# Decode attention plus a gated MLP on one core: four-head tiles in five places against eight-head tiles in three

## The chip, the cores and the metric

One core of a Trainium2 chip runs the whole program. The metric is device time in microseconds (us), the median of three executions; lower is better. The profile is one further execution, read with the chip's hardware profiler. Engines are called PE (matrix), PEld (its weight loads), DVE (vector), ACT (scalar), POOL and SP; SP is here only the queue that issues the large transfers.

## The reference, cut to what matters

Four batch rows, one new token each, D = 640, 32 heads of 128, caches of 4,096 positions, all in bfloat16.

```
xn = layernorm(x)                                  # x: 4 x 1 x 640
q  = (xn @ wq) per head                            # wq: 640 x 4096
p  = softmax(q . k_cache / sqrt(128))              # k_cache: 4 x 32 x 4096 x 128
o  = p . v_cache                                   # v_cache: the same shape
A  = o @ wo                                        # wo: 4096 x 640
z  = gelu(xn @ w_in);  z1, z2 = halves of z        # w_in: 640 x 1728
B  = (z1 * (w_sp * layernorm(z2) + b_sp)) @ w_out  # w_out: 864 x 640
out = x + A + B
```

The two caches are 134 MB each. With wq, wo and the MLP's weights 282 MB have to be read, and every byte of the caches is used once.

## The kernel before, in words

A tile is the K or the V cache of four heads of one batch row: 4 x 4,096 positions x 128, laid on 128 lanes as 128 positions of 128 values each, 32 KB a lane, 4 MB in all. A lane holds positions of one head only, 32 lanes a head. There are 32 tiles of K and 32 of V, in the order head group by head group, four batch rows within each. They share a pool of five places of 32 KB a lane (`KV_SLOTS`); wq and the MLP's weights use three of the five first. `loads` is the fixed order of the transfers on SP's queue, and `pump()` issues the next as soon as the tile that had its place has been used.

The loop over `i` (32 turns) is an order written out by hand for PE, DVE, ACT and SP. Turn i works on the scores of K tile i, on the softmax of tile i - 1 and on a V tile one or more turns behind:

- `stage_q(i + 2)` spreads the query of the four heads over the lanes: four matmuls into four groups of 32 lanes (L389), and an ACT copy (L397).
- `product` (DVE, L403) multiplies a quarter of the K tile by that query into a tile `prod`, `fold_half` (DVE, L415) adds the upper 64 values of each position to the lower 64 into a tile `folded`, `sums` (PE, L427) adds eight-value pieces of a half tile with eight matmuls by the identity, and `row_sums` (DVE, L438) adds the last eight.
- For the softmax `lane_max`, `turn_max`, `head_max` and `spread_max` carry the largest score of each head across the lanes, and `exps` (ACT, L480) makes one exponential a head, each on that head's own 32 lanes, into a tile `p_m` that was zeroed at the start. Each also gives the sum of its values.
- `weighted` (PE, L495) loads each of the 128 positions of the V tile as weights (128 x 128) and moves the four columns of `p_m` past them.
- After four batch rows `group_den`, `group_norm` and `group_proj` (L507 to L525) divide by the sums and multiply by that head group's rows of wo. wo comes in eight transfers (`load_wo`) of 1,280-byte runs, spread over the loop.

The scores tile `s_sb` has two buffers, so that the next tile's `row_sums` never meets the `exps` of the last. The last V tile comes in four pieces (`V_CUTS`).

Ahead of the loop wq is read in five transfers, four rows of each lane's five in one and the fifth row in four pieces, three of them spread (`SPREADS`, L96); then come w_in and w_out, and 160 matmuls by wq (L236) give the queries.

Of the kernel before, what the change touches and what calls it, by code (L numbers as in the profile page):

```python
# [15 lines left out]
KV_SLOTS = 5  # L16
EXTRA_K = (24, 28)
# [3 lines left out]
def kernel(  # L21
# [14 lines left out]
    nc = tc.nc  # L36
# [11 lines left out]
    HT = 4  # L48
# [4 lines left out]
    NQ = 4  # L53
    QC = NC // NQ
    HC = NC // 2
    HD2 = Dh // 2
    RW = 8
    SLOT = NC * Dh
    NFF = Fh // P
    NFC = NFF + 1  # L60
    FT = Fh - NFF * P
    NOH = D // 2

    const = ctx.enter_context(tc.tile_pool(name="const", bufs=1))
    kv = ctx.enter_context(tc.tile_pool(name="kv", bufs=KV_SLOTS))
    wop = ctx.enter_context(tc.tile_pool(name="wop", bufs=1))
    prod = ctx.enter_context(tc.tile_pool(name="prod", bufs=1))
    fold = ctx.enter_context(tc.tile_pool(name="fold", bufs=2))
    work = ctx.enter_context(tc.tile_pool(name="work", bufs=1))
    small = ctx.enter_context(tc.tile_pool(name="small", bufs=2))  # L70
    PSUM = bass.MemoryType.PSUM
    ps_s = ctx.enter_context(tc.tile_pool(name="ps_s", bufs=2, space=PSUM))
    ps_pv = ctx.enter_context(tc.tile_pool(name="ps_pv", bufs=2, space=PSUM))
    ps_m = ctx.enter_context(tc.tile_pool(name="ps_m", bufs=2, space=PSUM))
    ps_out = ctx.enter_context(tc.tile_pool(name="ps_out", bufs=1, space=PSUM))

    def slot(name):
        return kv.tile([P, SLOT], BF16, tag="kv", name=name)

    x_bf = const.tile([Bsz, D], BF16)
    nc.scalar.dma_start(out=x_bf[:], in_=A_x.flatten_outer_dims())

    wq_v = A_wq.rearrange("(p c) n -> p c n", c=DC)
    wq_parts = []
    t = slot("wq")[:, 0 : HT * HD].rearrange("p (c n) -> p c n", n=HD)
    nc.sync.dma_start(out=t, in_=wq_v[:, 0:HT, :])
    wq_parts += [(t, i) for i in range(HT)]
    assert DC == HT + 1  # L90
    SPREADS = (2, 4, 8)
    NW = HD // (len(SPREADS) + 1)
    t = slot("wq")[:, 0:HD]
    nc.sync.dma_start(out=t[:, 0:NW], in_=wq_v[:, HT, 0:NW])
    for g, k in enumerate(SPREADS, 1):
        nc.sync.dma_start(  # L96
            out=t[:, g * NW : (g + 1) * NW],
            in_=wq_v[:, HT, g * NW : (g + 1) * NW].rearrange("(b a) n -> a b n", a=k),
        )
    wq_parts.append((t.rearrange("p (c n) -> p c n", c=1), 0))  # L100
# [6 lines left out]
    w_sb = slot("w_sb")  # L107
# [15 lines left out]
    V_CUTS = (0, 64, 96, 112, NC)  # L123

    def load(which, i):
        cache, tiles = (A_k_cache, k_tiles) if which == "k" else (A_v_cache, v_tiles)
        t = slot("k_nat" if which == "k" else "v_nat")
        cuts = V_CUTS if (which, i) == ("v", NT - 1) else (0, NC)
        for c0, c1 in zip(cuts, cuts[1:]):
            nc.sync.dma_start(  # L130
                out=t[:, c0 * Dh : c1 * Dh], in_=kv_view(cache, i)[:, c0 * Dh : c1 * Dh]
            )
        tiles[i] = t[:].rearrange("p (c d) -> p c d", d=Dh)

    loads = [("k", 0), ("k", 1)]
    n_k = 2
    for i in range(NT):
        loads.append(("v", i))
        for _ in range(2 if i + 1 in EXTRA_K else 1):
            if n_k < NT:  # L140
                loads.append(("k", n_k))
                n_k += 1
    occupants = [("w", 0), ("w", 1), ("w", 2)] + loads
    used = set()
    n_loaded = [0]

    def pump():
        while n_loaded[0] < len(loads):
            at = n_loaded[0] + 3 - KV_SLOTS
            if at >= 0 and occupants[at] not in used:  # L150
                return
            load(*loads[n_loaded[0]])
            n_loaded[0] += 1

    wo_v = A_wo.rearrange("(j h p) n -> j p h n", p=P, h=HT)
    wo_tiles = {}

    def load_wo(j):
        wo_tiles[j] = wop.tile([P, HT, D], BF16, name="wo")
        if j == HG - 1:  # L160
            for hh in range(HT):
                nc.sync.dma_start(out=wo_tiles[j][:, hh, :], in_=wo_v[j][:, hh, :])
            return
        nc.sync.dma_start(out=wo_tiles[j][:], in_=wo_v[j])

    pump()


# [4 lines left out]
    nc.vector.tensor_copy(out=ident_f[:], in_=ident[:])  # L173
    ones_row = const.tile([1, P], FP32)
    nc.vector.memset(ones_row[:], 1.0)
    eps_tile = const.tile([P, 1], FP32)
    nc.vector.memset(eps_tile[:], eps)
    scale_row = const.tile([1, P], FP32)
    nc.vector.memset(scale_row[:], scale_qk)
    ones_sq = const.tile([P, P], FP32)  # L180
    nc.vector.memset(ones_sq[:], 1.0)

    NACC = 2
    p_m = [const.tile([P, NC, HT], BF16, name=f"pm{b}") for b in range(Bsz)]
    acc = [const.tile([P, HT, Bsz], FP32, name=f"acc{g}") for g in range(NACC)]
    for t in p_m + acc:
        nc.gpsimd.memset(t[:], 0.0)

# [5 lines left out]
    for i in range(NSTAT):  # L194
# [8 lines left out]
    xn_bf = work.tile([Bsz, D], BF16)  # L203
    nc.vector.tensor_scalar(
        out=xn_bf[:],
        in0=x_bf[:],
# [6 lines left out]
    xn_v = xn_bf[:].rearrange("b (p c) -> b c p", c=DC)  # L213
    NX = DC + len(SPREADS)
    xnT_ps = ps_m.tile([P, NX, Bsz], BF16, tag="m")
    for g, k in enumerate(SPREADS):
        xn_l = work.tile([Bsz, P], BF16, name=f"xn_l{g}")
        nc.vector.tensor_copy(
            out=xn_l[:].rearrange("b (a q) -> b a q", a=k),
            in_=xn_v[:, HT, :].rearrange("b (q a) -> b a q", a=k),  # L220
        )
        nc.tensor.transpose(
            out=xnT_ps[:, DC + g, :], in_=xn_l[:], identity=ident[:Bsz, :Bsz]
        )
# [4 lines left out]
    xnT = const.tile([P, NX, Bsz], BF16)  # L229
    nc.vector.tensor_copy(out=xnT[:], in_=xnT_ps[:])  # L230

    q_ps = ps_m.tile([P, H, Bsz], FP32, tag="m", name="q_ps")
    for h in range(H):
        for c in range(DC):
            t, i = wq_parts[c]
            nc.tensor.matmul(  # L236
                out=q_ps[:, h, :],
                lhsT=t[:, i, h * Dh : (h + 1) * Dh],
                rhs=xnT[:, c if c < HT or h * Dh < NW else DC + h * Dh // NW - 1, :],
                start=(c == 0),  # L240
                stop=(c == DC - 1),
            )
    qT = const.tile([P, H, Bsz], BF16)
    nc.vector.tensor_copy(out=qT[:], in_=q_ps[:])  # L244


# [16 lines left out]


    gm = {}
    for name in ("zz", "gw", "gt", "gz"):
        gm[name] = work.tile([P, 2, NFC, Bsz], FP32, name=name)
    nc.gpsimd.memset(gm["zz"][:], 0.0)
    gm["sq"] = work.tile([P, NFC, Bsz], FP32, name="sq")
# [4 lines left out]
    def gmlp():  # L274
        zz, gw, gt, gz, sq = (gm[n] for n in ("zz", "gw", "gt", "gz", "sq"))
        zT = ps_pv.tile([P, 2, NFC, Bsz], FP32, tag="pv", name="zT")
        for t in range(2):
# [13 lines left out]
        nc.vector.tensor_tensor(out=gw[:], in0=zz[:], in1=zz[:], op=ALU.mult)  # L291
        nc.vector.tensor_scalar(
            out=gw[:], in0=gw[:], scalar1=0.044715, scalar2=1.0, op0=ALU.mult, op1=ALU.add
        )
        nc.vector.tensor_tensor(out=gw[:], in0=gw[:], in1=zz[:], op=ALU.mult)
        nc.scalar.activation(
            out=gt[:], in_=gw[:], func=ACT.Tanh, scale=math.sqrt(2.0 / math.pi)
        )
        nc.vector.tensor_scalar(
            out=gt[:], in0=gt[:], scalar1=1.0, scalar2=0.5, op0=ALU.add, op1=ALU.mult  # L300
        )
        nc.vector.tensor_tensor(out=gz[:], in0=zz[:], in1=gt[:], op=ALU.mult)
        nc.vector.tensor_tensor(out=sq[:], in0=gz[:, 1, :, :], in1=gz[:, 1, :, :], op=ALU.mult)

        s_ps = ps_m.tile([1, 2 * Bsz], FP32, tag="m", name="ln_ps")
        for src, at in ((gz[:, 1, :, :], 0), (sq[:], Bsz)):
            for k in range(NFC):
                nc.tensor.matmul(
                    out=s_ps[:, at : at + Bsz],
                    lhsT=ones_sq[:, 0:1],  # L310
                    rhs=src[:, k, :],
                    start=(k == 0),
                    stop=(k == NFC - 1),
                )
# [5 lines left out]
        tmp_t = st[:, 4 * Bsz : 5 * Bsz]  # L320
        nc.vector.tensor_scalar(
            out=st[:, 0 : 2 * Bsz],
            in0=s_ps[:],
# [33 lines left out]
            out=sq[:],  # L357
# [5 lines left out]
            out=sq[:],  # L363
            in0=sq[:],
# [3 lines left out]
        nc.vector.tensor_tensor(out=gm["yT"][:], in0=gz[:, 0, :, :], in1=sq[:], op=ALU.mult)  # L368
# [12 lines left out]

    qbcs, scores, pvs = {}, {}, {}
    folds, sums_ps, maxes = {}, {}, {}

    def stage_q(i):
        hg, b = divmod(i, Bsz)
        qb_ps = ps_m.tile([P, Dh], FP32, tag="m", name="qbc_ps")
        for hh in range(HT):
            nc.tensor.matmul(  # L389
                out=qb_ps[hh * LN : (hh + 1) * LN, :],  # L390
                lhsT=qT[:, HT * hg + hh, b : b + 1].to_broadcast([P, LN]),
                rhs=ident[:],
                start=True,
                stop=True,
            )
        qbcs[i] = small.tile([P, Dh], BF16, name="qbc", bufs=3)
        nc.scalar.copy(out=qbcs[i][:], in_=qb_ps[:])  # L397

    prods = {}

    def product(i, q):
        t = prods[i, q] = prod.tile([P, QC, Dh], BF16, name="prod")
# [134 lines left out]
    def at(i, fn, *args):  # L537
        if 0 <= i < NT:
            fn(i, *args)
# [101 lines left out]
```

## Time and profile before

| what | value |
|---|---|
| median of three executions | 682.32 us (682.05 to 682.57) |
| profiled execution, first to last instruction (span) | 680.6 us |
| read from memory | 282.2 MB, 415 GB/s over the span |
| large transfers' share of 16 DMA engines | 97.9% |
| DVE busy | 507.6 us (75%) |
| PE busy | 394.1 us (58%), at a mean granted clock of 0.627 |
| ACT busy | 94.3 us (14%) |

The profiled execution gives its span alone; the median lies 1.7 us above it, which is what lies around the span. The page shows the span in 40 slices of 17.0 us. Only the first two and the last move clearly less than 419 to 433 GB/s. A line Lnnn is that of the kernel before unless it is said to be of the kernel after.

### The profile page before, as it was taken

What the parts mean: (1) busy time and instruction counts of PE and PEld (TensorE: products, weight loads), DVE (VectorE), ACT (ScalarE), POOL (GpSimd) and SP (SyncE); (2) the same over time, 40 slices, a digit from 0 to 9 for tenths busy, and PEclk for the clock granted to TensorE, in tenths of its full rate; (3) what the DMA queues carried; (4) which work ended last, traced back from release to release, by engine and by line L of the source; (5) the groups of instructions that cost most, each with busy time, mean ns of one, the idle gap of its engine ahead of it and who ended that gap; (6) DMA issues with size and microseconds to landing.
All of it is one profiled execution on the core that took longest, in us unless ns stands there. A gap on an engine that the chain in (4) does not pass through costs nothing.

```text
span 680.6 us, 11504 instructions
## 1 busy us (share of the span) xinstructions
PE 394.1 (58%) x5196; PEld 214.0 (31%) x5196; DVE 507.6 (75%) x436; ACT 94.3 (14%) x329; POOL 2.8 (0%) x13
## 2 busy tenths in 40 slices
PE   1234766684555666554565745566655557645486
PEld 1221333332223333322333322333333224323155
DVE  1059987778777778797777887777786999876950
ACT  0110211111110111111011111101111111110120
POOL 1000000000000000000000000000000000000000
PEclk9999566666566556566656665755565665656565
DMA  8999999999999999999999999999999999999993
GB/s 312 340 429 433 427 429 428 419 431 431 429 430 425 428 430 431 421 432 432 429 430 423 429 429 430 427 427 430 429 432 424 428 430 427 428 432 430 433 409 130
DMA packets 15082, 282.98 MB, mean 416 GB/s; under 512 B 1358, under 2 KB 5562, under 8 KB 6458
## 3 DMA queue, kind: packets, MB, share of 16 engines
q1 hardware_dynamic: 15014, 282.25, 97.9%
q8 instruction: 40, 0.66, 0.4%
q14 instruction: 8, 0.07, 0.0%
q10 hardware_dynamic: 20, 0.01, 0.0%
HBM read 282.24 MB, written 0.01 MB: 415 GB/s over the span
## 4 chain that ended last, share of the span: by engine, by line
DMA 55%; DVE 25%; PE 16%; SPq 2%; issue 1%; DVEq 0%
DMA k_nat<-in_A_k_cache_dram 55%; DVE prod L403 14%; PE s_ps L427 9%; DVE folded L415 7%; PE pv L495 6%; DVE s_sb L438 3%; SPq L96 2%; DVE m L447 1%; DVE nm L457 0%; PE qbc_ps L389 0%; PE den L507 0%; SPq L110 0%; PE out_ps L525 0%; DVE rden L511 0%; SPq L114 0%
## 5 line engine op out<-in xcount | busy, mean ns | idle before, releaser
L403 DVE TENSOR_TENSOR prod<-k_nat,qbc 128x4096 bf16<-128x4096 bf16 x128 | 292.7, 2287 | 78.4 <-DMA k_nat<-in_A_k_cache_dram 76.8
L427 PE MATMUL s_ps<-folded,ident 128*128 128x512 bf16 x512 | 226.0, 620 | 82.2 <-DVE folded L415 82.2
L415 DVE TENSOR_TENSOR folded<-prod 128x2048 bf16<-128x2048 bf16 x128 | 156.1, 1220 | 3.3
L427 PEld LDWEIGHTS <-ident 128*128 128x128 bf16 x512 | 71.1, 139 | 192.1 <-issue 191.3
L495 PE MATMUL pv<-pm,v_nat 128*128 128x4 bf16 x4096 | 111.2, 167 | 3.4 <-issue 3.4
L495 PEld LDWEIGHTS <-v_nat 128*128 128x128 bf16 x4096 | 108.8, 100 | 7.0 <-issue 4.1
L480 ACT ACTIVATE pm<-s_sb,nb 32x128 bf16<-32x128 f32 x128 | 73.9, 578 | 2.6
L452 PE MATMUL mT<-ident_f,m 128*1 128x128 f32 x32 | 11.3, 353 | 107.9 <-DVE m L447 107.9
L476 ACT COPY nb<-nb_ps 128x4 f32<-128x4 f32 x32 | 5.2, 162 | 468.7 <-PE nb_ps L468 468.7
L468 PE MATMUL nb_ps<-nm,scale_row 1*128 1x4 f32 x64 | 17.7, 345 | 58.5 <-DVE nm L457 58.5
L438 DVE TENSOR_REDUCE s_sb<-s_ps 128x64 f32<-128x512 f32 x64 | 43.6, 681 | 6.7 <-PE s_ps L427 3.7
L452 PEld LDWEIGHTS mT<-ident_f,m 128*1 128x1 f32 x32 | 2.5, 79 | 135.3 <-DVE m L447 98.8
L468 PEld LDWEIGHTS nb_ps<-nm,scale_row 1*128 1x128 f32 x64 | 15.6, 302 | 68.3 <-issue 57.3
L511 DVE RECIPROCAL rden<-den 128x16 f32<-128x16 f32 x8 | 2.1, 258 | 41.5 <-PE den L507 41.5
L480 ACT ACTIVATION_READ_ACCUMULATOR pm<-s_sb,nb 32x1 f32 x128 | 32.1, 251 | 0.0
L397 ACT CAST qbc<-qbc_ps 128x128 bf16<-128x128 f32 x32 | 8.4, 266 | 87.9 <-PE qbc_ps L389 87.9
L244 DVE CAST qT<-q_ps 128x128 bf16<-128x128 f32 x1 | 0.3, 292 | 23.3 <-PE q_ps L236 23.3
L236 PE MATMUL q_ps<-xnT,wq 128*128 128x4 bf16 x160 | 5.1, 167 | 18.0 <-DMA wq<-in_A_wq_dram 18.0
L389 PEld LDWEIGHTS <-qT 128*32 128x32 bf16 x128 | 3.4, 99 | 24.2 <-issue 23.7
L236 PEld LDWEIGHTS <-wq 128*128 128x128 bf16 x160 | 4.7, 104 | 18.7 <-DMA wq<-in_A_wq_dram 18.7
L447 DVE TENSOR_REDUCE m<-s_sb 128x1 f32<-128x128 f32 x32 | 9.2, 286 | 1.1
L457 DVE TENSOR_REDUCE nm<-mT 1x4 f32<-1x128 f32 x32 | 8.7, 272 | 0.6 <-PE mT L452 0.6
(72 smaller groups left out, 59.7 us busy)
## 6 DMA issues: line engine op xcount, KB each, us to landing
k_nat<-in_A_k_cache_dram SPq DMA_DIRECT2D x32, 4096.0 KB, 42.1
v_nat<-in_A_v_cache_dram SPq DMA_DIRECT2D x31, 4096.0 KB, 35.0
wo<-in_A_wo_dram SPq DMA_DIRECT2D x7, 640.0 KB
wq<-in_A_wq_dram SPq DMA_DIRECT2D x1, 4096.0 KB
w_sb<-in_B_w_in_dram SPq DMA_DIRECT2D x1, 2160.0 KB
v_nat<-in_A_v_cache_dram SPq DMA_DIRECT2D x1, 2048.0 KB
wq<-in_A_wq_dram SPq DMA_DIRECT2D x4, 256.0 KB, 12.6
v_nat<-in_A_v_cache_dram SPq DMA_DIRECT2D x1, 1024.0 KB
```

The lines of the kernel that those rows point to most:

```text
L96: nc.sync.dma_start(out=t[:, g * NW : (g + 1) * NW], in_=wq_v[:, HT, g * NW : (g + 1) * NW].rearrange("(b a) n -> a b n", a=k),)
L236: nc.tensor.matmul(out=q_ps[:, h, :], lhsT=t[:, i, h * Dh : (h + 1) * Dh], rhs=xnT[:, c if c < HT or h * Dh < NW else DC + h * Dh // NW - ...
L403: nc.vector.tensor_tensor(out=t[:], in0=k_tiles[i][:, q * QC : (q + 1) * QC, :], in1=qbcs[i][:, None, :].to_broadcast([P, QC, Dh]), op=ALU ...
L415: nc.vector.tensor_tensor(out=folds[i, half][:, part * QC : (part + 1) * QC, :], in0=t[:, :, 0:HD2], in1=t[:, :, HD2:Dh], op=ALU.add,)
L427: nc.tensor.matmul(out=s[:], lhsT=ident[:], rhs=t[:, :, g * RW : (g + 1) * RW], start=(g == 0), stop=(g == n - 1),)
L438: nc.vector.tensor_reduce(out=scores[i][:, half * HC : (half + 1) * HC], in_=sums_ps.pop((i, half))[:], axis=AX.X, op=ALU.add,)
L447: nc.vector.tensor_reduce(out=m1[:], in_=scores[i][:], axis=AX.X, op=ALU.max)
L452: nc.tensor.transpose(out=mT[:], in_=maxes[i][:], identity=ident_f[:])
L457: nc.vector.tensor_reduce(out=nm[:], in_=maxes[i][:].rearrange("a (h p) -> a h p", h=HT), axis=AX.X, op=ALU.max, negate=True,)
L468: nc.tensor.matmul(out=nb_ps[:], lhsT=scale_row[:], rhs=maxes[i][:], start=True, stop=True)
L480: nc.scalar.activation(out=pm[ps, :, hh], in_=s_sb[ps, :], func=ACT.Exp, bias=nb[ps, hh : hh + 1], scale=scale_qk, accum_out=a[ps, hh, b : ...
L495: nc.tensor.matmul(out=pvs[hg][:, :, b], lhsT=v_nat[:, c, :], rhs=pm[:, c, :], start=(c == 0), stop=(c == NC - 1),)
```

## The change

The tile becomes eight heads: 64 KB a lane, 256 positions a lane, 16 lanes a head, 8 MB; there are 16 of K and 16 of V. The pool of five becomes two places for K and one for V, of 64 KB a lane each. wq has the first K place at the start, the MLP's weights have the V place, and at the end the last V tile takes a K place and wo takes the V place.

- `product` and `fold` write over the K tile itself; the unit stays a quarter of a tile, so each instruction is twice as long, and `sums` and `row_sums` work on quarters.
- One exponential a head now runs over all 128 lanes. A bias of -1e30 on the lanes of other heads (`off`, added by the new `bias`) makes their values zero, so no tile has to be zeroed.
- `weighted` loads the probabilities as weights (four positions x eight heads = 32 columns) and moves V past them, 512 columns a matmul, into four groups of 32 lanes in turn: 64 matmuls a tile, of which only the blocks of equal position are wanted. `take` (ACT) copies the result out, and `diag` (PE) picks the wanted blocks with a 0/1 matrix `pick` and adds them up over the four batch rows of a head group.
- `group_rows` (DVE) divides by the sums and spreads the heads, `group_turn` (PE, ACT) turns the result for the projection by wo. All four `group_proj` stand after the last tile, since wo now comes last, in runs of 10 KB, the last group in four pieces (`WO_CUTS`).
- wq comes in one transfer of 40 KB runs. The copies of the query that the spread pieces needed are gone.
- `s_sb` has one buffer, so `row_sums(i, 0)` waits until `exps(i - 1)` has read the old scores. `load_v(i)` is issued after `weighted(i - 1)`, `load_k(i + 2)` after the last `sums` of tile i. PE's `weighted` stands behind `sums(i, 2)` and ahead of `sums(i, 3)`.

PE's program shrinks from 10,185 to 3,854 rows, DVE's from 437 to 291.

```diff
-KV_SLOTS = 5
-EXTRA_K = (24, 28)
+OFF = -1.0e30
...
-    HT = 4
+    HT = 8
...
-    kv = ctx.enter_context(tc.tile_pool(name="kv", bufs=KV_SLOTS))
-    wop = ctx.enter_context(tc.tile_pool(name="wop", bufs=1))
-    prod = ctx.enter_context(tc.tile_pool(name="prod", bufs=1))
-    fold = ctx.enter_context(tc.tile_pool(name="fold", bufs=2))
+    kp = ctx.enter_context(tc.tile_pool(name="kp", bufs=2))
+    vp = ctx.enter_context(tc.tile_pool(name="vp", bufs=1))
...
+    wq_t = k_slot("wq")[:, 0 : DC * HD].rearrange("p (c n) -> p c n", n=HD)
+    nc.sync.dma_start(out=wq_t, in_=A_wq.rearrange("(p c) n -> p c n", c=DC))
...
+    def product(i, u):
         nc.vector.tensor_tensor(
-            out=t[:],
-            in0=k_tiles[i][:, q * QC : (q + 1) * QC, :],
-            in1=qbcs[i][:, None, :].to_broadcast([P, QC, Dh]),
+            out=part(i, u),
+            in0=part(i, u),
+            in1=qbcs[i][:, None, :].to_broadcast([P, UC, Dh]),
             op=ALU.mult,
         )
...
+    def fold(i, u):
+        t = part(i, u)
         nc.vector.tensor_tensor(
+            out=t[:, :, 0:HD2], in0=t[:, :, 0:HD2], in1=t[:, :, HD2:Dh], op=ALU.add
+        )
...
+    def row_sums(i, u):
+        if u == 0:
+            scores[i] = small.tile([P, NC], FP32, name="s_sb", bufs=1)
...
+    def bias(i):
+        nb = small.tile([P, HT], FP32, name="nb")
+        nc.vector.scalar_tensor_tensor(
+            out=nb[:], in0=maxes[i][:], scalar=scale_qk, in1=off[:], op0=ALU.mult, op1=ALU.add
+        )
...
+        for h in range(HT):
             nc.scalar.activation(
-                out=pm[ps, :, hh],
-                in_=s_sb[ps, :],
+                out=pm[:, :, h],
+                in_=s_sb[:],
                 func=ACT.Exp,
-                bias=nb[ps, hh : hh + 1],
+                bias=nb[:, h : h + 1],
                 scale=scale_qk,
-                accum_out=a[ps, hh, b : b + 1],
+                accum_out=a[:, b, h : h + 1],
             )
...
     def weighted(i, c0=0, c1=NC):
+        if c0 == 0:
+            pvs[i] = ps_pv.tile([P, CB * Dh], FP32, tag="pv", name="pv")
+        v_nat, pm = v_tiles[i], pms[i]
+        for n in range(c0 // CB, c1 // CB):
+            j = n % CG
+            nc.tensor.matmul(
+                out=pvs[i][j * GW : (j + 1) * GW, :],
+                lhsT=pm[:, n * CB : (n + 1) * CB, :],
+                rhs=v_nat[:, n * CB : (n + 1) * CB, :],
+                start=(n < CG),
+                stop=(n >= NB - CG),
+            )
...
+        for i in range(NT):
+            product(i, 0)
+            fold(i, 0)
+            at(i - 1, row_sums, NU - 1)
+            at(i - 1, lane_max)
+            group(i - 2, group_rows)
+            sums(i, 0)
+            at(i - 1, turn_max)
+            group(i - 2, group_turn)
+            product(i, 1)
+            at(i - 1, head_max)
+            at(i - 1, spread_max)
+            fold(i, 1)
+            at(i - 1, bias)
+            at(i - 1, exps)
+            at(i + 1, stage_q)
+            sums(i, 1)
+            row_sums(i, 0)
+            product(i, 2)
+            fold(i, 2)
+            sums(i, 2)
+            row_sums(i, 1)
+            at(i - 1, weighted)
...
+                load_v(i, v_slot("v_nat"))
...
+            at(i - 1, take)
+            product(i, 3)
+            fold(i, 3)
+            sums(i, 3)
+            row_sums(i, 2)
+            if i + 2 < NT:
+                load_k(i + 2)
...
+            at(i - 1, diag)
+            group(i - 1, group_den)
...
+        for c0, c1 in zip(V_CUTS, V_CUTS[1:]):
+            weighted(L, c0, c1)
+        take(L)
+        group_den(HG - 1)
+        group_proj(0)
+        diag(L)
+        group_rows(HG - 1)
+        group_proj(1)
+        group_turn(HG - 1)
+        group_proj(2)
+        for j0, j1 in zip(WO_CUTS, WO_CUTS[1:]):
+            group_proj(HG - 1, j0, j1)
```

## The prediction, made blind

> **What bounds the kernel now.** I read the page's engine and slice rows first, then its groups, then the timeline of one turn, of the start and of the end.
>
> ```profile
> PE 394.1 (58%) x5196; PEld 214.0 (31%) x5196; DVE 507.6 (75%) x436; ACT 94.3 (14%) x329; POOL 2.8 (0%) x13
> ...
> DMA  8999999999999999999999999999999999999993
> GB/s 312 340 429 433 427 429 428 419 431 431 429 430 425 428 430 431 421 432 432 429 430 423 429 429 430 427 427 430 429 432 424 428 430 427 428 432 430 433 409 130
> ...
> q1 hardware_dynamic: 15014, 282.25, 97.9%
> ```
>
> The transfers bound it: their row is full in all slices but the ends, at some 430 GB/s, while DVE has a quarter of the span free. So the question is whether three places keep the queue as full as five did, and what start and end cost.
>
> ```profile
> 333.31 2.29 DVE L403 TENSOR_TENSOR prod<-k_nat,qbc 128x4096 bf16<-128x4096 bf16 x1 [3.55 <-DMA k_nat<-in_A_k_cache_dram]
> 335.64 1.22 DVE L415 TENSOR_TENSOR folded<-prod 128x2048 bf16<-128x2048 bf16 x1
> 336.78 0.68 DVE L438 TENSOR_REDUCE s_sb<-s_ps 128x64 f32<-128x512 f32 x1
> 337.50 0.29 DVE L447 TENSOR_REDUCE m<-s_sb 128x1 f32<-128x128 f32 x1
> ...
> 340.91 0.16 ACT L476 COPY nb<-nb_ps 128x4 f32<-128x4 f32 x1 [14.86 <-PE nb_ps L468]
> 341.11 0.59 ACT L480 ACTIVATE pm<-s_sb,nb 32x128 bf16<-32x128 f32 x1
> ...
> 341.44 0.26 ACT L480 ACTIVATION_READ_ACCUMULATOR pm<-s_sb,nb 32x1 f32 x1
> 341.71 0.58 ACT L480 ACTIVATE pm<-s_sb,nb 32x128 bf16<-32x128 f32 x1
> ...
> 352.74 2.29 DVE L403 TENSOR_TENSOR prod<-k_nat,qbc 128x4096 bf16<-128x4096 bf16 x1 [3.56 <-DMA k_nat<-in_A_k_cache_dram]
> ...
> 360.79 3.57 PE L427 MATMUL s_ps<-folded,ident 128*128 128x512 bf16 x8 [0.49 <-DVE folded L415]
> ...
> 364.29 0.29 PE L389 MATMUL qbc_ps<-ident,qT 128*32 128x128 bf16 x4
> ...
> 676.48 1.23 PE L525 MATMUL out_ps<-wo,o_n 128*4 128x320 bf16 x8 [0.27 <-DVE o_n L516]
> ```
>
> Columns: start, length, engine, line. DVE waits for K at 333.31 and at 352.74: a K and a V tile (8.39 MB) arrive every 19.43 us, so a new tile of 8.39 MB takes 19.43. Exponentials follow each other every 0.60, the read of the sum included. Eight 512-column matmuls take 3.57, 0.427 apart. Two rows show column groups working together: four 128-column matmuls of L389 in 0.29, and eight 320-column ones of L525 in 1.23, which one after another at 0.267 would be 2.1.
>
> ```profile
> 364.00:365.00 1.00, 1.00 (x24) 0.60 (x24) 0.32 (x1) 0.27 (x1) 0.00 (x0) 0.78 1.07 428
> 365.00:366.00 1.00, 1.00 (x46) 1.00 (x44) 0.00 (x0) 0.00 (x0) 0.00 (x0) 1.00 1.01 424
> ...
> 12.00:28.00 16.00, 4.05 (x127) 3.73 (x128) 0.00 (x0) 0.00 (x0) 0.00 (x0) 1.00 0.94 270
> ```
>
> Of these stretches the last three columns are clock, DMA share and GB/s. The clock goes to 1.0 just after the sums of 360.79. In the clock records it is 0.5 or 1.0 in stretches of 3.41 us; in the main loop all windows at least 0.79 filled with sums were followed by 1.0, none under 0.75 without L495 in them. From 12 to 28 us only 270 GB/s moved: SP is held for 11.2 us by the spread pieces of wq (L96), and w_in follows only at 12.9.
>
> ```profile
> 1.65 11.20 SPq L96 DMA_DIRECT2D wq<-in_A_wq_dram  x3
> 12.89 1.30 SPq L110 DMA_DIRECT2D w_sb<-in_B_w_in_dram  x1
> ...
> 678.28 0.30 SPq L610 DMA_DIRECT2D out_dram<-res  x1
> ```
>
> **A turn of the new loop**, from the landing of K tile i (time 0). From L403 and L415, 2,048 more elements cost 1.07 us and 0.15 is fixed, so a product takes 4.42 and a fold 2.29; with the overlaps of the rows above, starts lie 4.46 and 2.27 apart. In place neither the element count nor the step within a row changes, so I add nothing; if products lost the pairwise rate, each would take 4.27 more (a rival). Product, fold, row_sums 0.72, lane_max 0.33, product, head_max 0.20, fold and bias end at 14.75. Eight exponentials: 128 more elements at ACT's step, bounded by nothing (period 0.60) and by the whole ACTIVATE doubling (1.18). The read of the sum begins 0.33 after the start, so little of the 0.58 is the elements; I take 0.71, near the lower end, and they end at 20.4. Only then may DVE's `row_sums(i, 0)` go, because `s_sb` has one buffer: this new wait holds DVE some 5.7 us, and behind it are products 2 and 3. PE's `stage_q` and `sums(i, 1)` stand behind the same exponentials, harmlessly. The second fold after it ends at 27.9, `sums(i, 2)` at 31.4, then `weighted(i - 1)`: 64 x 512 columns in four groups. All overlapped at half clock it is 16 x 0.427 = 6.8, at full clock 3.4, in series 27.3. L525's pairs start 0.266 apart, 320 columns at half clock, with the next weights already in; so I take full overlap, and since the eight sums just ahead fill a window, a clock that rises about 0.9 us into it: 4 us. It ends at 35.5. SP's issue to the first byte took 1.05 at the start (0.73 to 1.77 in the packet records), so V tile i starts at a = 36.6.
>
> DVE's own turn is 35.8, under 38.9, so it hides. On SP, K tile i + 2 stands behind V tile i. So a turn lasts 38.9 (two transfers) or (a + 38.9) / 2, whichever is more: V may start up to 38.9 after K's landing, and the margin is 2.3 us. This is the whole risk: where a exceeds 38.9, queue time is lost in every turn. What else is new lies beside this at nothing: `take` (ACT, some 0.6 from L607's 0.42 for 320 columns) and `diag` come after V's issue, ACT has 7 and PE some 20 of 38.9 us, and the zeroing of `p_m`, the three query copies and the 4,096 small matmuls that go were not late for anything. Every fourth turn `group_rows` adds 1.5 on DVE (1,024 elements at L438's rate, one per cycle, and a small one), and the turn before it ends with the reciprocal of `group_den`, which waits on PE for `sums(i, 3)` and `diag` and holds the next product by 0.3 to 2.7. Three times that eats the margin: 2.4 together.
>
> **Start.** Bytes ahead of K tile 0's last: wq 5.24, MLP 3.32, K 8.39 MB. At 430 GB/s from 1.8 us, with 0.8 for the slow first packets, it lands at 42; if w_in and w_out come as slowly as in the row of 12 to 28 us, at 46.6. I take 44.3. Turn 0 has no softmax: 28.7. Turn 1 has: V tile 1 starts 36.6 later, at 109.6. By then K tile 2 has long landed (44.3 + 3 x 19.43 = 102.6): the queue stands still 7 us, the price of three places. A restart costs 0.7.
>
> **The rest.** From V tile 1 to K tile 15 are 26 transfers: 505.2. Fetches of PE's instructions (40 packets of 16 KB, some 1.07 us each, on a few DMA engines) fall with PE's rows from 10,185 to 3,854: about 1.6 on the worst engine. So K tile 15 lands at 109.6 + 0.7 + 505.2 + 1.6 + 2.4 = 619.5.
>
> **End.** Turn 15: `weighted(14)` ends at 35.5, the last sums at 37.4, softmax as at the old end (2.9 from row_sums to the first exponential), exponentials to 45.9, `weighted(15)` from a cold clock 5.6, a projection 1.2, `diag` 1.7, `group_rows` 1.6, turn 0.7, two projections 2.4: 59.1; casts, issue and landing of the result as before (677.74 to 680.6, 2.9): 62.0. At half clock throughout it is 3 more; I add 0.8. wo lands near 51 and hides. Removed wo transfers gain 2 to 3 us of queue time by their longer runs, which the queue's total contains; the end hides it.
>
> Span: 619.5 + 62.8 = 682.3, against 680.6 now. With 1.7 around it: **684.0**, 0.25% slower. What the weights and wo save, the empty queue at V tile 1 and an end with a whole tile's softmax behind the last K give back. About 0.2% (1.4 us) is what a measurement here can tell from no change.
>
> **Rivals.** *Faster*: the start is clean (42.0) and 64 KB runs save packet gaps: 32 KB packets start 1.213 us apart; half the gaps of at most 9 ns are 0.07 a tile, 1.9 in all. 684.0 - 2.3 - 1.9 = 679.8; with no loss in the group turns 677.4. For it: the wq rows at the start move 430. Against it: w_in's slowness is not shown to come from the spread pieces.
>
> *Slower, the margin goes*: it decides at a = 38.9. At a period of 1.18 the exponentials end 3.8 later and a = 40.4; at half clock a = 39.4. Then (40.4 + 38.9) / 2 = 39.65, 0.75 more in each of 13 turns, three group turns 2 more each, V tile 1 and the end 3 to 4 more each: 684 + 10 + 6 + 7 = 707; with half clock alone near 700. Against it: the sums ahead of `weighted` fill the window.
>
> *Slower, weights are not loaded ahead*: each round of four waits for its loads, 0.11 (four of 99 ns, L389, overlapped): `weighted` takes 1.8 more, a = 38.4, still under 38.9, but the three group turns lose 1.8 more, V tile 1 and the end 1.8 each: 684 + 9 = 693. Row L525 speaks against it. [...] L525's 82 ns loads, same rows, cost nothing visible.
>
> *Far slower*: four streams of different data do not overlap at all. 64 matmuls, part at full clock, take some 16 to 27 us, a = 49 to 60, a turn 44 to 49: 750 to 850. L525 shows two different streams, L389 four of the same; four different ones no row shows.
>
> *It does not do what it says*: in place the products lose the pairwise rate; DVE's turn becomes 35.8 + 4 x 4.27 = 52.9 and the time about 900.
>
> **Chances.** Forecast (681 to 690) 0.50, faster 0.20, margin 0.14, loads 0.08, no overlap 0.05, in place 0.03. By sign: of the forecast 0.03 lies below 681, 0.17 within 0.2%, 0.30 above; of the faster rival 0.17 and 0.03. So faster 0.20, same 0.20, slower 0.60. The range leaves out the last two rivals, the upper half of the margin and the lowest of the faster: 678 to 702.
>
> **What the new profile would show.** Right: DMA slices full but for a dip near 103 to 110 us; the first product near 44 us; K's landings 38.9 apart; DVE waiting some 5.7 us a turn for ACT at `row_sums`; `weighted` in about 4 us; 14 us or more between the last wo packet and the end. Wrong: gaps in the DMA row in every turn (a over 38.9), `weighted` over 7 us, products over 4.6 us, or a first product at 42 with full slices all through.

## The result, and the profile after

The changed kernel takes 722.95 us (median of 4 runs, 720.85 to 724.88) against 682.18 us for the kernel before (4 runs): a ratio of 1.060, 95% interval 1.058 to 1.062. It is slower, as forecast, but by 41 us and not by 2, beyond the 702 that the range reached to. The profiled execution has a span of 720.5 us (before: 680.6). From here on, line numbers are those of the changed kernel: L402 is `product`, L411 `fold`, L431 `row_sums`, L480 `exps`, L495 `weighted`, L128 and L122 the loads of V and K.

From the page of the changed kernel: engines, the DMA row and its GB/s in 40 slices, and SP's queue.

```profile
PE 310.7 (43%) x2089; PEld 129.2 (18%) x2089; DVE 491.3 (68%) x291; ACT 172.7 (24%) x317; POOL 1.0 (0%) x8
...
DMA  9999958999899997999899997999999897999981
GB/s 379 444 426 440 419 233 350 407 456 415 354 407 407 416 455 295 407 463 411 350 407 466 409 451 303 411 408 437 433 387 429 353 463 295 407 463 407 395 361 66
...
q1 hardware_dynamic: 6456, 282.24, 91.9%
```

Read it against the rows of before. The first slices are faster (379 and 444 GB/s where 312 and 340 stood), so the start did get clean. The dip at slices 6 and 7, 90 to 126 us, is the empty queue ahead of V tile 1. But the row does not fill up after it: slices of 295 to 355 GB/s come back every few slices to the end, and the queue is busy 91.9% where it was 97.9%. PE works less than before and DVE too; only ACT rose, from 94.3 to 172.7 us, with 12 instructions fewer. One turn in the timeline of the changed kernel shows the rest:

```profile
320.79 4.42 DVE L402 TENSOR_TENSOR k_nat<-k_nat,qbc 128x8192 bf16<-128x8192 bf16 x1 [3.53 <-DMA k_nat<-in_A_k_cache_dram]
...
335.43 1.43 ACT L480 ACTIVATE pm<-s_sb,nb 128x256 bf16<-128x256 f32 x1 [18.19 <-DVE nb L468]
336.36 0.49 ACT L480 ACTIVATION_READ_ACCUMULATOR pm<-s_sb,nb 128x1 f32 x1
336.38 1.60 ACT L480 ACTIVATE pm<-s_sb,nb 128x256 bf16<-128x256 f32 x1
337.50 0.49 ACT L480 ACTIVATION_READ_ACCUMULATOR pm<-s_sb,nb 128x1 f32 x1
337.52 1.60 ACT L480 ACTIVATE pm<-s_sb,nb 128x256 bf16<-128x256 f32 x1
...
344.82 0.69 DVE L431 TENSOR_REDUCE s_sb<-s_ps 128x64 f32<-128x512 f32 x1 [9.43 <-ACT pm L480]
...
355.72 4.40 PE L495 MATMUL pv<-v_nat,pm 128*32 128x512 bf16 x64
...
359.95 4.41 DVE L402 TENSOR_TENSOR k_nat<-k_nat,qbc 128x8192 bf16<-128x8192 bf16 x1
360.18 0.33 SPq L128 DMA_DIRECT2D v_nat<-in_A_v_cache_dram  x1
361.99 0.33 SPq L122 DMA_DIRECT2D k_nat<-in_A_k_cache_dram  x1
```

The bias is ready 14.6 us into the turn, as forecast. Then the exponentials follow each other every 1.14 us (the first after 0.95), not every 0.71, and the eight with their sums take 9.4 us. The row of an ACTIVATE (1.60) is longer than that because it overlaps the one ahead of it; what a series of exponentials costs is this time from start to start, called the period below. DVE's `row_sums` stands behind them for 9.43 us (5.7 forecast). `weighted` takes 4.40 (4 forecast). V is issued 39.4 us into the turn, and DVE's own turn is 39.16 long, with no wait for K at its end. Both are now above the 38.9 us that two transfers take.

In the sum of the prediction the 38.2 us that the span is too long lie in three places. The first byte of V tile 1 moves at 114.0 (its landing of 133.35 less one transfer of 19.36) instead of 110.3: 3.7. From there to the landing of K tile 15 at 651.8 it takes 537.8 instead of 509.2: 28.6. The end takes 68.7 instead of 62.8: 5.9.

### The profile page after: what moved, and what is told of

It reads as the page before. It is cut to its first block, busy times and chain, and to the rows that moved or that the text cites. A ratio compares the mean times of both kernels' runs of the same rounds, so it can differ in the third digit from the quotient of the medians.

```text
span 720.5 us, 4972 instructions
## 1 busy us (share of the span) xinstructions
PE 310.7 (43%) x2089; PEld 129.2 (18%) x2089; DVE 491.3 (68%) x291; ACT 172.7 (24%) x317; POOL 1.0 (0%) x8
## 3 DMA queue, kind: packets, MB, share of 16 engines
q1 hardware_dynamic: 6456, 282.24, 91.9%
## 4 chain that ended last, share of the span: by engine, by line
DVE 37%; DMA 34%; ACT 14%; PE 12%; issue 1%; SPq 0%; DVEq 0%
DMA k_nat<-in_A_k_cache_dram 34%; DVE k_nat L402 22%; ACT pm L480 14%; DVE k_nat L411 11%; PE s_ps L420 6%; PE pv L495 5%; DVE s_sb L431 3%; DVE wide L537 1%; DVE m L440 1%; PE out_ps L564 0%; PE o_ps L515 0%; DVE nm L450 0%; DVE o_n L533 0%; DVE nb L468 0%; SPq L109 0%
## 5 line engine op out<-in xcount | busy, mean ns | idle before, releaser
L402 DVE TENSOR_TENSOR k_nat<-k_nat,qbc 128x8192 bf16<-128x8192 bf16 x64 | 282.6, 4416 | 28.1 <-DMA k_nat<-in_A_k_cache_dram 28.1
L420 PE MATMUL s_ps<-k_nat,ident 128*128 128x512 bf16 x512 | 198.9, 559 | 181.3 <-DVE k_nat L411 181.3
L480 ACT ACTIVATE pm<-s_sb,nb 128x256 bf16<-128x256 f32 x128 | 149.8, 1582 | 223.3 <-DVE nb L468 223.3
L411 DVE TENSOR_TENSOR k_nat<-k_nat 128x4096 bf16<-128x4096 bf16 x64 | 146.4, 2287 | 1.7
L431 DVE TENSOR_REDUCE s_sb<-s_ps 128x64 f32<-128x512 f32 x64 | 43.9, 686 | 143.5 <-ACT pm L480 141.5
L480 ACT ACTIVATION_READ_ACCUMULATOR pm<-s_sb,nb 128x1 f32 x128 | 63.0, 493 | 0.0
L505 ACT COPY e<-pv 128x512 f32<-128x512 f32 x16 | 9.4, 586 | 220.9 <-PE pv L495 215.3
L495 PE MATMUL pv<-v_nat,pm 128*32 128x512 bf16 x960 | 61.6, 414 | 0.0
L495 PEld LDWEIGHTS <-pm 128*32 128x32 bf16 x1024 | 27.2, 105 | 53.6 <-issue 23.9
L515 PE MATMUL o_ps<-e,pick 128*32 128x128 f32 x128 | 16.9, 275 | 0.0
L515 PEld LDWEIGHTS o_ps<-e,pick 128*32 128x32 f32 x128 | 12.8, 109 | 6.4 <-issue 6.4
L495 PE MATMUL pv<-v_last,pm 128*32 128x512 bf16 x64 | 5.5, 519 | 9.7 <-ACT pm L480 9.7
## 6 DMA issues: line engine op xcount, KB each, us to landing
w_sb<-in_B_w_out_dram SPq DMA_DIRECT2D x1, 960.0 KB, 22.6
```

Source lines behind the costliest of these rows:

```text
L402: nc.vector.tensor_tensor(out=part(i, u), in0=part(i, u), in1=qbcs[i][:, None, :].to_broadcast([P, UC, Dh]), op=ALU.mult,)
L411: nc.vector.tensor_tensor(out=t[:, :, 0:HD2], in0=t[:, :, 0:HD2], in1=t[:, :, HD2:Dh], op=ALU.add)
L420: nc.tensor.matmul(out=s[:], lhsT=ident[:], rhs=t[:, :, g * RW : (g + 1) * RW], start=(g == 0), stop=(g == n - 1),)
L431: nc.vector.tensor_reduce(out=scores[i][:, u * UC : (u + 1) * UC], in_=sums_ps.pop((i, u))[:], axis=AX.X, op=ALU.add,)
L480: nc.scalar.activation(out=pm[:, :, h], in_=s_sb[:], func=ACT.Exp, bias=nb[:, h : h + 1], scale=scale_qk, accum_out=a[:, b, h : h + 1],)
L495: nc.tensor.matmul(out=pvs[i][j * GW : (j + 1) * GW, :], lhsT=pm[:, n * CB : (n + 1) * CB, :], rhs=v_nat[:, n * CB : (n + 1) * CB, :], sta ...
```

## The experiments

The theory: an exponential costs more than was taken, because `pm[:, :, h]` is written with 16 bytes from one value to the next (8 bytes before, with four heads). So V goes out late, the queue runs dry, and with one place for V nothing else can fill it. The rivals: something else makes the exponentials long (lanes, values, underflow); three places lose the time whatever they cost; DVE's own turn and not V's issue is the bound.

**E1, adjacent writes.** The table that picks the wanted blocks changes with it (left out here).

```diff
...
-        pm = pms[i] = pmp.tile([P, NC, HT], BF16, tag="pm", name="pm")
+        pm = pms[i] = pmp.tile([P, HT, NC], BF16, tag="pm", name="pm")
-                out=pm[:, :, h],
+                out=pm[:, h, :],
...
-        v_nat, pm = v_tiles[i], pms[i]
+        v_nat = v_tiles[i].rearrange("p (q n) d -> p n q d", n=NB)
+        pm = pms[i][:].rearrange("p h (q n) -> p n (h q)", n=NB)
-                lhsT=pm[:, n * CB : (n + 1) * CB, :],
-                rhs=v_nat[:, n * CB : (n + 1) * CB, :],
+                lhsT=pm[:, n, :],
+                rhs=v_nat[:, n, :, :],
...
```

> The changed kernel with one edit: each head's exponentials are written to 256 adjacent values instead of every eighth; the weighted sums read their weights and values with a constant step instead, same instructions in the same order. Theory (the step of 16 bytes makes an exponential slow): its period falls from 1.13 to 0.65-0.80 us, V is issued some 3 us earlier in a turn (36.0-36.5 instead of 39.4), the queue no longer empties every second turn, turns go from 41 to 39, 683-690 us. Rival 1 (the length is due to 128 lanes, 256 elements, or values of e^-1e30): period stays 1.13, 720-725 us. Rival 2 (three places, restarts and engine skew lose the time whatever the exponentials cost): period falls but the time stays over 710.

681.06 us, 0.998 of before (0.996 to 0.999): 42 us gained, to just below the 683 to 690 expected. The groups of this kernel (busy us, mean ns of one), its GB/s row, and two exponentials of one series:

```profile
L480 ACT ACTIVATE pm<-s_sb,nb 128x256 bf16<-128x256 f32 x128 | 63.1, 494 | 261.6 <-DVE nb L468 261.6
...
L480 ACT ACTIVATION_READ_ACCUMULATOR pm<-s_sb,nb 128x1 f32 x128 | 23.9, 186 | 0.0
...
GB/s 372 440 434 433 434 375 310 433 431 433 430 433 433 426 430 387 433 434 433 430 433 433 427 433 388 433 433 434 433 434 433 433 433 434 387 441 430 416 418 203
...
320.80 0.49 ACT L480 ACTIVATE pm<-s_sb,nb 128x256 bf16<-128x256 f32 x1
...
321.29 0.49 ACT L480 ACTIVATE pm<-s_sb,nb 128x256 bf16<-128x256 f32 x1
```

An ACTIVATE went from 1582 to 494 ns, the read of its sum from 493 to 186, the period from 1.14 to 0.49, where 0.65 to 0.80 was expected. V is now issued 33.0 to 34.6 us into a turn, 36.5 with a group, and the queue is full between the dip ahead of V tile 1 and three others, four turns apart. The weights, now read at a step, load in 170 instead of 105 ns, but the 64 matmuls hardly take longer (3.7 to 4.9 us by turn, 3.6 to 4.9 in the changed kernel). The step of the writes was the cause, and three places as such do not lose the time.

**E2, other values.**

```diff
-OFF = -1.0e30
+OFF = -1.0
```

> The changed kernel with a bias of -1 in place of -1e30 for the lanes of other heads (leaves out the masking, so the sums are others). If an exponential is slow because seven of eight values underflow, its period falls from 1.13 to about 0.7 and the time to 683-690; by the theory of the step nothing changes: 1.13 and 720-725 us.

One run: 724.55 us, and again 1582 ns for an ACTIVATE. Underflow is out.

```profile
L480 ACT ACTIVATE pm<-s_sb,nb 128x256 bf16<-128x256 f32 x128 | 149.8, 1582 | 223.9 <-DVE nb L468 223.9
```

**E3, V early.** The order of PE and SP alone; the exponentials stay slow.

```diff
+            at(i - 1, weighted)
+            if i == 0:
+                pass
+            elif i < NT - 1:
+                load_v(i, v_slot("v_nat"))
+            else:
+                load_wo()
             sums(i, 2)
             row_sums(i, 1)
-            at(i - 1, weighted)
-            if i == 0:
-                pass
-            elif i < NT - 1:
-                load_v(i, v_slot("v_nat"))
-            else:
-                load_wo()
```

> The changed kernel with the weighted sums of the tile before, and behind them V's load, moved ahead of the third sums on PE and SP; exponentials unchanged. Theory (the late issue of V empties the queue): V is issued near 29 us into a turn instead of 39.4, V tile 1 no longer waits, turns fall from 41 to DVE's own 39.2, the end stays 68.7: 687-692 us, although the exponentials' period stays 1.13 and DVE still waits 9.4 for them. Rival (three places, restarts and skew lose it anyway): over 710. Rival (DVE's own turn with its wait is what sets the turn): gain under 10 us, 713-723.

714.38 us, 1.046 of before (1.044 to 1.048): only 8.6 us gained, so the rival named last was right and 687 to 692 was wrong. V is issued 31 to 34 us into a turn and no longer binds. The chain of waits of this kernel, by engine, and a stretch of its timeline at a group's end:

```profile
DVE 64%; ACT 21%; DMA 6%; issue 4%; PE 4%; SPq 0%; DVEq 0%
```

```profile
228.53 0.68 DVE L431 TENSOR_REDUCE s_sb<-s_ps 128x64 f32<-128x512 f32 x1
...
233.25 0.16 DVE L529 RECIPROCAL rden<-den 32x1 f32<-32x1 f32 x1 [4.04 <-PE den L525]
233.33 4.42 DVE L402 TENSOR_TENSOR k_nat<-k_nat,qbc 128x8192 bf16<-128x8192 bf16 x1
```

DVE, with ACT behind it, is the chain: plain turns last 39.15, the turn that ends with a group's reciprocal 43.4 to 44.0, and the one after it 41.5. A group thus costs 6.5 to 7.2 us, and nothing hides it once DVE is the bound. That is what the expectation had left out.

**E4, DVE busy meanwhile.** The first row sums go behind the third fold, so that DVE works while the exponentials run.

```diff
             sums(i, 1)
-            row_sums(i, 0)
             product(i, 2)
             fold(i, 2)
+            row_sums(i, 0)
```

> The changed kernel with the first row sums of a turn moved behind the third fold on DVE, so that DVE has products to do while the exponentials run; exponentials unchanged at 1.13. Theory: DVE's wait falls from 9.4 to 2-3 us, V is issued 5-7 us earlier (32.5-34.5 into a turn), the queue stays full from V tile 1 on, the end is 3-5 us shorter: 679-686 us. Rival (restarts and skew of three places): over 705.

685.11 us, 1.003 of before (1.002 to 1.004), within the expected 679 to 686. DVE's wait for ACT falls from 9.4 to 2.8 us a turn and V is issued at 33.0 to 36.5:

```profile
289.28 0.69 DVE L431 TENSOR_REDUCE s_sb<-s_ps 128x64 f32<-128x512 f32 x1 [2.81 <-ACT pm L480]
```

The exponentials are as slow as ever (1589 ns): 38 of the 41 us come back by hiding them.

**E12, V late, DVE fast.** E1, and in its order:

```diff
-            at(i - 1, weighted)
-            if i == 0:
-                pass
-            elif i < NT - 1:
-                load_v(i, v_slot("v_nat"))
-            else:
-                load_wo()
-            at(i - 1, take)
             product(i, 3)
             fold(i, 3)
             sums(i, 3)
             row_sums(i, 2)
+            at(i - 1, weighted)
+            if i == 0:
+                pass
+            elif i < NT - 1:
+                load_v(i, v_slot("v_nat"))
+            else:
+                load_wo()
+            at(i - 1, take)
```

> The version with adjacent writes (681 us), with the weighted sums and V's load moved the other way: behind the fourth sums of the turn, so that V is issued near 39.5 us into a turn, as in the changed kernel, while DVE keeps its short turn of some 33. Theory (V's issue by itself empties the queue: in the runs so far, V's landing follows K's by 19.36 where V is issued over 4 us ahead of K's landing, by 21.8 at the same moment, 24 at 2 us behind it): two turns take 39.5 + 42.5 = 82, K tile 15 lands at 640-652 instead of 620: 700-713 us. Rival (DVE's turn of 39.15 was the cause, and the late V costs nothing by itself): 680-686.

729.88 us, 1.068 of before (1.065 to 1.071), beyond the 713 expected; V came out at 40.5 to 41.8, a microsecond later than planned, and at 42.7 to 43.9 with a group. The page of this kernel:

```profile
DMA  9999948999799995999899996999979898899965
GB/s 376 442 450 414 447 187 343 407 458 407 289 446 418 436 428 230 458 407 457 350 400 407 401 450 249 457 403 444 418 292 457 364 444 349 349 454 414 426 268 224
```

These are the holes of the changed kernel, though DVE waits for K here (94.1 us in all). At three group ends the reciprocal also waits 8.8 to 9.5 us for the late `weighted` and `diag`; after two of them K came later still. So a late V empties the queue by itself (E12), and a DVE turn of 39.15 with its group stops is slow by itself (E3). In the changed kernel the slow exponential causes both.

**E7, E11, E10 and E8, the price of a step.** The eight heads of a chunk of four positions are interleaved by G (the table of the wanted blocks changes with it, left out here): G = 4 gives 8 bytes from value to value (E7), 2 gives 4 bytes (E11), 1 gives runs of four adjacent values, a run every 64 bytes (E10). E8 is the kernel before with `p_m` as `[P, HT, NC]`.

```diff
...
-        pm = pms[i] = pmp.tile([P, NC, HT], BF16, tag="pm", name="pm")
+        pm = pms[i] = pmp.tile([P, NB, 8 // G, CB, G], BF16, tag="pm", name="pm")
-                out=pm[:, :, h],
-                in_=s_sb[:],
+                out=pm[:, :, h // G, :, h % G],
+                in_=s_sb[:].rearrange("p (n c) -> p n c", c=CB),
...
-                lhsT=pm[:, n * CB : (n + 1) * CB, :],
+                lhsT=pm[:, n],
...
```

> The changed kernel with the eight heads of a chunk of four laid as two blocks of four heads, so that an exponential writes its values 8 bytes apart (fours, then a jump) instead of 16; all else the same. If the price grows with the step, its period lies between the 0.49 of adjacent writes and 1.13, near 0.75-0.85, and the time is 684-700 us; if any step away from adjacent costs the whole, it stays at 1.13 and 720-725.

> The changed kernel with an exponential's values 4 bytes apart (pairs of heads interleaved). By the rows so far the price per value is 0.75 ns adjacent, 2.0 at 8 bytes, 5.0 at 16. If it grows in proportion to the step beyond 2 bytes, 4 bytes give 1.1-1.3 ns a value and a period of 0.53-0.60; if any step costs the 8-byte price, 0.65. Time 681-687 either way.

> The changed kernel with an exponential's values in runs of four adjacent ones (8 bytes), a run every 64 bytes; 32 weights of a chunk stay adjacent. If the price goes by the step from one value to the next, the period is near that of adjacent writes (0.49-0.60) and the time 680-686; if it goes by the bytes spanned (64 a run, as with a step of 16), it stays at 1.13 and the time at 720-725.

> The kernel before with its exponentials (32 lanes, 128 values) written adjacent instead of 8 bytes apart. If the row that the prediction scaled up from (period 0.60) already held a price for the step, the period falls to 0.33-0.40; if 0.60 is a fixed cost, it stays. The time stays at 680-684 either way: transfers bound that kernel.

| kernel | lanes x values | bytes from value to value | ACTIVATE, ns | read of the sum, ns | period, us (median) | time, us |
|---|---|---|---|---|---|---|
| changed | 128 x 256 | 16 | 1582 | 493 | 1.13 | 722.95 |
| E7 | 128 x 256 | 8 | 816 | 237 | 0.64 | 686.62 (one run) |
| E11 | 128 x 256 | 4 | 560 | 175 | 0.51 | 679.82 (one run) |
| E10 | 128 x 256 | runs of four | 494 | 186 | 0.49 | 680.12 (one run) |
| E1 | 128 x 256 | 2 | 494 | 186 | 0.49 | 681.06 |
| before | 32 x 128 | 8 | 578 | 251 | 0.60 | 682.18 |
| E8 | 32 x 128 | 2 | 398 | 184 | 0.51 | 682.46 (one run) |

The groups of E7, of E11, of E10 and of E8:

```profile
L480 ACT ACTIVATE pm<-s_sb,nb 128x256 bf16<-128x256 f32 x128 | 84.3, 816 | 246.7 <-DVE nb L468 246.7
```

```profile
L480 ACT ACTIVATE pm<-s_sb,nb 128x256 bf16<-128x256 f32 x128 | 66.7, 560 | 258.6 <-DVE nb L468 258.6
```

```profile
L480 ACT ACTIVATE pm<-s_sb,nb 128x256 bf16<-128x256 f32 x128 | 63.1, 494 | 257.4 <-DVE nb L468 257.4
```

```profile
L480 ACT ACTIVATE pm<-s_sb,nb 32x128 bf16<-32x128 f32 x128 | 51.0, 398 | 2.3
```

From the two adjacent rows, (494 - 398) / 128 = 0.75 ns a value and 302 fixed, an estimate. With that, in the rows of an ACTIVATE, 8 bytes cost 2.2 ns a value on 32 lanes and 2.0 on 128 lanes, 4 bytes 1.0, 16 bytes 5.0: at one step the number of lanes changes next to nothing, and the step changes most. The period says it more plainly, since rows overlap: with adjacent writes it is 0.51 at 128 values and 0.49 at 256, so that there the values cost nothing, and at 16 bytes it is 1.13. E10 shows that it is not the bytes spanned, since its runs are 64 bytes apart and as cheap as adjacent values (494 ns).

Three of the expectations missed the period. E7's 0.64 is below the 0.75 to 0.85 expected, E11's 0.51 just below 0.53 to 0.60 (its time of 679.82 just below 681). E8's 0.51 lies between its two cases, 0.33 to 0.40 if the step were in the 0.60 and 0.60 if it were not: the old row held a price for its step, but only 0.09 of the period.

The largest jump of an ACTIVATE lies between 8 and 16 bytes (816 to 1582 ns), and at 8 bytes it was not yet down to the adjacent row (816 against 494). Why the step costs this, no run shows.

**E5 and E9, both causes away, and the end.** E5 is E1 and E3 together. E9 adds to it the last K tile in quarters:

```diff
-        nc.sync.dma_start(out=t[:], in_=kv_view(A_k_cache, i))
+        cuts = range(0, NC + 1, UC if i == NT - 1 else NC)
+        for c0, c1 in zip(cuts, cuts[1:]):
+            nc.sync.dma_start(
+                out=t[:, c0 * Dh : c1 * Dh], in_=kv_view(A_k_cache, i)[:, c0 * Dh : c1 * Dh]
+            )
```

> Both edits of the earlier runs together: exponentials written to adjacent values, and the weighted sums with V's load ahead of the third sums. Theory (each takes one of the two causes away: the late issue of V, and DVE's own turn of 39.15 with its wait): V is issued near 28 into a turn, V tile 1 before or just as K tile 2 lands, so that the queue does not run dry there either (4 us saved against adjacent writes alone) nor after the group turns (two us each in three places): K tile 15 lands at 605-612, then 57-59: 664-673 us. Rival (engine skew and not the issue of V is behind the turns of 40 to 41 that are left): 675-681.

> The version with adjacent writes and early V, and K tile 15 loaded in four quarters instead of one transfer, so that turn 15 starts on its first quarter. In the run without it DVE stood idle 4.8 us ahead of turn 15 and K tile 15 landed whole at 608.5, 59.4 before the end of the span. Theory (DVE's turn 15 and the tail behind it set the end): turn 15 starts 4-5 us earlier and so does the end: 664.5-667 us. Rival (the end is set by V tile 15 and wo behind it on the queue): no gain, 669-671.

E5: 670.21 us, 0.982 of before (0.980 to 0.983). V tile 1 is issued at 99.65, ahead of K tile 2's landing, and K tile 15 lands at 608.5, 43 us earlier than in the changed kernel. E9: 665.71 us, 0.976 of before (0.974 to 0.977), the fastest version. Turn 15 starts at 604.0 instead of 608.6, and the span ends at 663.7 instead of 667.9; its chain of waits now ends with V tile 15 and wo on the queue, so by that chain more of DVE's time would no longer help. The page of E9 shows no hole left:

```profile
DMA  9999999999999999999999999999999999999996
...
q1 hardware_dynamic: 6888, 282.24, 98.9%
```

**E6, the start alone.** In the kernel before, the fifth rows of wq as one transfer:

```diff
-    SPREADS = (2, 4, 8)
...
+    SPREADS = ()
     t = slot("wq")[:, 0:HD]
...
+    nc.sync.dma_start(out=t, in_=wq_v[:, HT, :])
...
```

> The kernel before with one part of the change alone: the fifth rows of wq come in one transfer of 8 KB runs instead of one plain and three spread pieces. If the spread pieces (11.2 us of SP at the start, then slow packets) make the slow start, K tile 0 lands near 35 instead of 45.5 and, since the queue is full to the end, all of it shows at the end: 671-674 us. If the slowness has another cause: 680-683.

676.80 us, 0.991 of before (0.990 to 0.993). K tile 0 lands at 34.7 instead of 45.5. The stretch that moved 270 GB/s in the kernel before, in E6 (the last three columns are clock, DMA share, GB/s):

```profile
12.00:28.00 16.00, 9.70 (x266) 9.07 (x266) 2.13 (x12) 3.25 (x5) 0.00 (x0) 1.00 1.03 428
```

The spread pieces were the slow start. But of the 10.8 us at the first landing only 5.8 reach the end, so that the time lies between the 671 to 674 and the 680 to 683 expected. The single landings say why. A tile lands in 16 parts, and counts as landed with the last. The three spread transfers land in 2, 4 and 8 parts, and some parts of what follows come late: in E8, whose transfers are those of the kernel before, the last part of K tile 0 comes 8.0 us after the first, in E6 1.9. Against E8, E6's parts of K tile 0 land 6.2 us earlier on average (33.3 for 39.5), and those of the last large transfer 6.3 (663.6 for 669.9). Nothing is lost inside the loop; the rest of the 10.8 was the lag of the last part alone. Of the 17 us that E9 gains, 5.8 can thus be had in the kernel before.

## Why the prediction was wrong, step by step

**The exponential's price** is the term that failed: "I take 0.71, near the lower end". Measured: 1.14, almost the upper bound of 1.18. The sum had a price for twice the values and none for the step of `pm[:, :, h]`, which the change doubles from 8 to 16 bytes; it put the step at nothing without a reason. E7 parts the two: with twice the values at the old step the period is 0.64, so for the values alone 0.71 was even a little too much, and the other 0.49 is the doubled step. The reason given, that the read of the sum begins 0.33 after the start, could not see it: in the changed kernel that read begins 1.12 after its start. At a price near the one taken (E7) the sum comes close: V tile 1's first byte at 109.4 (110.3 forecast), K tile 15 at 624.3 (619.5), an end of 60.4 (62.8), 686.62 us (684.0). That it is only 2.6 off is partly luck, since 4.8 too little up to K tile 15 meets 2.4 too much at the end.

That the kernel came out slower, as forecast, supports the forecast little: it had 2 us for that, and 38 of the 41 measured come from this term, since hiding it (E4) gives them back.

**"V may start up to 38.9 after K's landing"** failed too, and is why the rival *the margin goes* had the mechanism and a = 40.4 right but 707 for 723. It counts an empty queue as lost only from the moment that the last byte of K is in, and it takes 1.05 us from the issue of V to its first byte. The traces (the changed kernel, E1, E3, E4, E7), by V's issue against K's last landing:

| V issued | V lands after K, us |
|---|---|
| over 4.2 us ahead | 19.36 in most, 20.9 at worst |
| 2.6 to 4.1 ahead | 19.4 to 21.9 |
| 0.8 to 2.4 ahead | 19.4 to 22.1 |
| at the same time | 21.8 |
| 0.7 to 2.7 behind | 22.6 to 24.7 |

The single landings of the changed kernel say where the 4 us come from. A tile lands in 16 parts. Where a transfer is issued at least 2.1 us before the first part of the tile ahead has landed (19 times), its own first part lands 19.3 to 19.5 us behind that one. Where it is issued 0.6 us before it or later (11 times, all of them V), its first part lands 21.1 to 21.3 us after the issue. So the queue loses whatever V's issue comes later than 1.9 us (21.24, the median, less 19.36) ahead of the first part, and the last part lands 0.5 to 2.8 us behind the first. Together that is 2.4 to 4.7 us ahead of the last landing. For the 1.9 the forecast had, at V tile 1 alone, 1.05 to the first byte and 0.7 for a restart, an estimate (in the kernel before the first 16 packets of 32 KB took 1.28 to 2.33 us, later ones 1.21).

K tiles land 38.7 apart at best, so a safe limit for V's issue is some 34.4 us after K's landing (4.3 less), not the 37.9 that a = 38.9 means. The forecast's own issue at 35.5 was already past it; it had no margin of 2.3 us. For the changed kernel, from V's issue at 360.18 to K's use at 402.67 there are 42.5 us; two turns thus take 39.4 + 42.5 = 81.9 and not 40.4 + 38.9 = 79.3.

**DVE's turn**, "35.8, under 38.9, so it hides": 39.16. Its wait for the exponentials is 3.7 us longer than forecast (9.43 for 5.7), and the rest of the turn 0.4 shorter. **Group turns**, "2.4 together": 6.5 to 7.2 each where DVE is the bound (E3). The reciprocal waited 2.4 to 3.3 us in the changed kernel and 4.0 to 4.7 in E3 (0.3 to 2.7 taken), and `group_rows` took 2.3 (1.5 taken, an estimate from the 0.68 us of L438's 512 values in the kernel before; the 1,024 values of its second instruction took 1.95). With DVE's short turn (E5) they hide.

**The end**, 62.8 forecast and 68.7 measured: two sets of eight exponentials stand in it, each 3.7 us longer. With E1's they took 57.8.

**Right**: the clean start (first product at 44.02, forecast 44.3, and E6 shows the spread pieces as its cause), though the number is partly luck: the forecast was the middle between a clean start at 42 and a slow one at 46.6, and what came was the clean one, with the first part of K tile 0 in at 42.3 and the last 1.7 later; products and folds in place (4.42 and 2.29, both as taken: 0.52 ns more an element, as before, where the f32 maxima take 1.05, 286 ns for 128 values before and 420 for 256 after); the queue empty ahead of V tile 1; V's issue waiting on `weighted`; four streams in one array at once (64 matmuls in 4.40, against 4). The rival *weights are not loaded ahead* did not come: loads of 105 ns, and in E1 even of 170, left `weighted` at 3.6 to 4.9 us, while 64 loads one after another would take 6.7 to 10.9.

## What to carry to other kernels

A write's step belongs in the price of an instruction (1582 ns for an exponential at 16 bytes, 494 with adjacent values): when a tile's inner dimension grows, look at how many bytes lie between the values that one instruction writes, and keep them adjacent or in short runs (E10 costs one rearrangement and keeps the weights adjacent too). A buffer with one place must be asked for by when its next transfer has to be *issued*, which here was some 4 us before the last byte of the transfer ahead. And where the bounds of one term (0.60 to 1.18 here) hold the point at which a rival decides (1.00 by the forecast's own limit, a margin of 2.3 us over eight exponentials above 0.71), one look at what sets that term is worth more than the rest of the sum.

## What the runs showed of the hardware

Not expected: the row of an ACTIVATE that writes 256 bf16 values 16 bytes apart is 3.2 times as long as that of the adjacent one (1582 against 494 ns), the read of its sum grows with it (493 against 186 ns), and a series of them has 2.3 times the period (1.13 against 0.49). A transfer of 8.39 MB issued into a queue that has run dry lands 21.7 to 22.0 us after its issue in the changed kernel, where one behind another takes 19.36, and even an issue 2 us ahead of the last landing mostly comes too late; the 16 landings of K tile 0 in the changed kernel lie between 42.3 and 44.0 us, so some parts are in up to 1.7 us before the last one. Where the queue was full throughout, such a lag stayed: in E8 the last part lands 8.0 us behind the first at K tile 0 and 9.4 at the last large transfer.
